# Last expert's second GEMM by seven products of halves, and S4 over 8 blocks of 256 samples

## The chip, the cores and the metric

The kernel runs on one core of one Trainium2 chip. The metric is the device time of one execution in microseconds. TensorE (PE) multiplies, VectorE (DVE) and ScalarE (ACT) do element-wise work, and GpSimd (POOL) and SyncE (SP) issue most DMAs. Each engine works through its own instructions in program order.

## The reference

The input x (2048 tokens by 512) is normalised to xn. The output is x plus a long convolution of xn (S4) plus a mixture of 8 experts on xn, in which all 8 experts are used for every token (top-8 of 8):

```python
def _A_ref(u, A_re, A_im, B_re, B_im, C_re, C_im, log_dt, Dskip):
    ...
    K = jnp.einsum("dn,dnl,dn->dl", Cc, P, dB).real      # 512 channels, 2048 samples, N = 128
    ...
    return y + u * Dskip                                  # y: causal convolution of u with K
def _B_ref(x, w_gate, w1, w2):
    ...
    for e in range(E):                                    # E = 8, D = 512, F = 1792
        h = _silu(xf @ w1[e]) @ w2[e]
        out = out + w * h                                 # w: softmax gate of the expert
x = A_u
xn = _layernorm(x, axis=-1)
return x + _A_ref(xn, ...) + _B_ref(xn, B_w_gate, B_w1, B_w2)
```

## The kernel before, in words

Each fp32 operand of a GEMM is split into a high and a low fp16 part, and each product is three fp16 matmuls (high·high, high·low, low·high). ACT makes the high part, and DVE the low part from it.

The work runs over experts e = 0..7, token blocks tb = 0..3 of 512 tokens, and four groups d of F (`DQS`: three groups of two pairs `pr`, one group of one pair; a pair is 256 of the 1792 columns). One (e, tb, d) is a call of `block`, which has four turns (`slot`, s = 0..3), so that a block of tokens has 16 turns.

- **First GEMM** (`product`, L1371, result `hb`): already seven products of halves per pair, 128x256 matmuls. Between them ACT copies one PSUM tile into another, which then accumulates on: `S.copy(B, A)` after turn 0 (L1605), `S.copy(C, B)` after turn 1 (L1615). Two of the four quarters of the result are finished by a copy to SBUF (`keep`, L1600) and an adding DMA on POOL's queue (`add`, L1571).
- **Activation** (`activate`): ACT takes the silu of a quarter (L1387) and makes the high part `ahl` (L1391); DVE makes the low part (L1400). Then the quarter stands in the list `units`.
- **Second GEMM** (`pop`, L1354 to L1356, result `y`): a unit is 2 x 3 matmuls of 128x512. `slot` takes `pops` units a turn from the list, behind the first GEMM's products of that turn. Four PSUM banks y0..y3 hold the four 128-token rows of a token block, and `evacuate` scales them by the gate and adds them to DRAM (`oacc`) by an adding DMA.
- **Weights** (`work_on`): list of steps that load, sum and split the next expert's w1 and w2, in the turns of the last token block of an expert and after it.
- **S4** runs beside all this. The 2048 samples of 16 channels (a chunk; 32 chunks) are 16 blocks of 128 samples. Per chunk: DVE builds tables (`s4_tables`, L769 to L775) from a basis made every second chunk (`s4_basis`), PE makes the kernel's samples (`s4_kernel`, L787), PE transforms kernel and input along the 128 samples (`s4_kf` L858, `s4_uf` L845), DVE multiplies and sums over the pairs of blocks (`s4_conv`, L884 to L898), PE transforms back (`s4_back`, L918), ACT reads it (`s4_out`, L925). DVE's share of it is issued by a budget: in each turn (`bg_run`) as many steps as 0.92 of the planned PE time leaves, less what DVE has otherwise. PE's share follows at fixed distances in turns (`until`, `hold`). What is not issued by the first turn of (7, 3), that is expert 7 and its last token block, is issued there in one go (`bg_until("s4")`), since its result is added from that block on (`s4_final`).
- **End**: after the last `block` the remaining units are popped, and `evacuate` combines the last four rows with what was loaded from `oacc` and sends them out by two queues.

The order of all instructions is written out by the program itself (a manual schedule): a turn, a list or a budget decides what is issued next, and the chip then runs each engine's instructions in that order.

Of the kernel before, what the change touches and what calls it, by code (L numbers as in the profile page):

```python
# [18 lines left out]
P = 128  # L19
# [14 lines left out]
def s4_moe_kernel(  # L34
# [205 lines left out]
    def x_sums(g, a):  # L240
# [90 lines left out]
    def x0_high(k):  # L331
        hi = xs_["hi"] = sb.tile([P, 4, TH], F16, tag="ta", name=f"x0h{k}", bufs=1)
# [51 lines left out]
    def gates_squares(row):  # L384
        gsq = sb.tile([P, KT * E], F32, tag="s4p1", bufs=1, name="gsq")
        S.activation(gsq, wgt.rearrange("p k e -> p (k e)"), AF.Square, accum_out=row)

    def gates_split():
# [3 lines left out]
        wgf = sb.tile([P, 6, E], F32, tag="s4p2", bufs=1, name="wgf")  # L392
# [142 lines left out]

    class Item:


        def __init__(self, load, steps, ready):
            self.load, self.steps, self.ready, self.raw, self.at = load, steps, ready, None, 0  # L540
            self.sums, self.n = len(steps) == 3, len(steps)
# [3 lines left out]
    live = {"n": 0, "tw": False}  # L545
# [4 lines left out]
    def piece_w1(e, pr, ready, raw=None):  # L550
# [6 lines left out]
        it.raw, it.made = raw, (e, "w1", pr)  # L557
        return it
# [6 lines left out]
    def piece_end(e, w, n, ready):  # L565
# [9 lines left out]
        def can_go():  # L575
            if "at" not in st:
                return ready()
            return now() > st["at"] + 1 and bank_free() and now() + 1 not in turns
# [18 lines left out]
    def can(it):  # L597
# [5 lines left out]
        if it.sums and len(it.steps) == it.n:  # L603
            return not live["tw"]
# [4 lines left out]
    def work_on(limit):  # L609
        while limit > 0:  # L610
# [15 lines left out]
            if it.sums and len(it.steps) == it.n:  # L626
                live["tw"], it.at = True, now()
# [6 lines left out]
            if low:  # L634
                lows.append((low, last, it.sums and last, it.made))
# [7 lines left out]
    def work_lows():  # L643

        while lows:
# [5 lines left out]
            if sums:  # L651
                live["tw"] = False
# [5 lines left out]
    ZSH = 18  # L658

    def s4_dft_load():  # L660
        s4["dft"] = sb.tile([P, 4, P], F32, tag="tb", name="dft", bufs=1)
        nc.sync.dma_start(s4["dft"], dft)

    def s4_dft():

        dftt = s4["dft"]
        times(dftt[:, 2:4, :], dftt[:, 2:4, :], DSH)
        V.tensor_copy(dfth[:, 0], dftt)
        V.tensor_tensor(dfth[:, 1], dftt, dfth[:, 0], op=ALU.subtract)

    def s4_dt():
        xx = [sb.tile([P, D], F32, tag=t, name=f"dtx{n}", bufs=1) for n, t in enumerate(("k4", "ta", "tt"))]
# [3 lines left out]
    upad = cp.tile([P, 2, DC, NI + 1], F32, name="upad")  # L676
# [4 lines left out]
    def s4_raw(g):  # L681
        raw = sb.tile([P, 6, GD], F32, tag="s4raw", name=f"s4raw{g}", bufs=2)
# [3 lines left out]
    def s4_basis(g):  # L686
# [3 lines left out]
        wv = sb.tile([P, 2, GD], F32, tag="s4w", name=f"s4w{g}", bufs=2)  # L690
        db = sb.tile([P, 2, GD], F32, tag="s4db", name=f"s4db{g}", bufs=1)
        p1 = sb.tile([P, 2, GD], F32, tag="s4p1", name=f"s4p1{g}", bufs=1)
        p2 = sb.tile([P, 2, GD], F32, tag="s4p2", name=f"s4p2{g}", bufs=1)
        at = sb.tile([P, 2, GD], F32, tag="s4at", name=f"s4at{g}", bufs=1)
# [12 lines left out]
        n4 = [P, 2, NK, DC]  # L707
# [6 lines left out]
        f = sb.tile(n4, F32, tag="b0", name=f"bf{g}", bufs=1)  # L714
        r = sb.tile(n4, F32, tag="b1", name=f"br{g}", bufs=1)
        x = sb.tile(n4, F32, tag="b2", name=f"bx{g}", bufs=1)
        zr = sb.tile(n4, F32, tag="zr", name=f"zr{g}", bufs=1)
        zi = sb.tile([P, 2] + n4[1:], F32, tag="zi", name=f"zi{g}", bufs=1)
# [23 lines left out]
        s4["basis", g] = (wv, zr, zi)  # L742
        yield 2 * tt_(352) + 0.3

    def s4_tables(c):
        g, h = c // 2, c % 2
        wv, zr, zi = s4["basis", g]
        tb = sb.tile([P, 2, 3, DC, 32], F32, tag="tb", name=f"tb{c}", bufs=1)
# [3 lines left out]
        for st in range(6):  # L752
# [9 lines left out]
            n4 = [P, 2, nn, L]  # L762
            zrv = zr[:, h, k0:k0 + ns, :].rearrange("p k d -> p (k d)").unsqueeze(1).unsqueeze(3).to_broadcast(n4)
            ziv = zi[:, :, h, k0:k0 + ns, :].rearrange("p c k d -> p c (k d)").unsqueeze(3).to_broadcast(n4)
            ta = sb.tile([P, 1024], F32, tag="ta", name=f"ta{c}_{st}", bufs=1)[:, :2 * nn * L]
            ta = ta.rearrange("p (c n l) -> p c n l", c=2, n=nn)
            tt = sb.tile([P, 1024], F32, tag="tt", name=f"tt{c}_{st}", bufs=1)[:, :2 * nn * L]
            tt = tt.rearrange("p (c n l) -> p c n l", c=2, n=nn)
            V.tensor_tensor(ta, tin, zrv, op=ALU.mult)  # L769
            if st > 2:  # L770
                yield tt_(2 * nn * L)
            V.tensor_tensor(tt, tin[:, ::-1], ziv, op=ALU.mult)
            if st > 2:
                yield tt_(2 * nn * L)
            V.tensor_tensor(tout, ta, tt, op=ALU.add)  # L775
            yield (1 if st > 2 else 3) * tt_(2 * nn * L) + 0.5 * (st == 0)
# [15 lines left out]
    def s4_kernel_out(c):  # L792
        ksb = sb.tile([P, 4, 4, NI], F32, tag="ksb", name=f"ksb{c}", bufs=1)
# [5 lines left out]
        kt = sb.tile([P, DC, NI], F32, tag="kt", name=f"kt{c}", bufs=1)  # L799
# [7 lines left out]
    def s4_kscale(c):  # L807


        ks = s4["ks", c] = sb.tile([P, 2], F32, tag="ksc", name=f"ksc{c}", bufs=4)  # L810
        pow2_scale(ks[:, 0:1], s4["kst", c], f"k{c}")
        pow2_inverse(ks[:, 1:2], ks[:, 0:1], ZSH - DSH)

    def s4_khigh(c):
        kh = s4["kh", c] = sb.tile([P, 2, DC * NI], F16, tag="kh", name=f"kh{c}", bufs=1)
# [8 lines left out]
    def s4_uload(c):  # L824

        uc = sb.tile([P, NI, DC], F32, tag="uc", name=f"uc{c}", bufs=1)
        nc.sync.dma_start(uc, xnd[:, :, c * DC:(c + 1) * DC])
        s4["uc", c] = uc.rearrange("p i d -> p d i")

    def s4_uhigh(c):  # L830
        uh = s4["uh", c] = sb.tile([P, 2, DC, NI], F16, tag="uh", name=f"uh{c}", bufs=1)
# [6 lines left out]

    def s4_uf(c):
        uh = s4["uh", c]  # L840
        take_bank()
        uf = ps_s.tile([P, 2, DC, NI], F32, tag="s4", name=f"uf{c}")
        for a in range(2):
            for n, (x, y) in enumerate(((0, 0), (1, 0), (0, 1))):
                T.matmul(uf[:, a].rearrange("p d i -> p (d i)"), dfth[:, x, a, :], uh[:, y].rearrange("p d i -> p (d i)"),  # L845
                         start=(n == 0), stop=(n == 2))
        clock["pe"] += 0.66
# [4 lines left out]
    def s4_kf(c):  # L852
        take_bank()
        kf = ps_s.tile([P, 2, DC, NI], F32, tag="s4", name=f"kf{c}")
        kh = s4["kh", c]
        for a in range(2):
            for n, (x, y) in enumerate(((0, 0), (1, 0), (0, 1))):
                T.matmul(kf[:, a].rearrange("p d i -> p (d i)"), dfth[:, x, 1 - a, :], kh[:, y], start=(n == 0), stop=(n == 2))  # L858
        clock["pe"] += 0.66
        k4 = sb.tile([P, 4, DC, NI], F32, tag="k4", name=f"k4{c}", bufs=1)  # L860
        S.copy(k4[:, 0:2].rearrange("p a d i -> p (a d i)"), kf.rearrange("p a d i -> p (a d i)"))
        bank["at"] = now()
        s4["k4", c] = k4

    def s4_conv(c):

        up, k4 = upad, s4["k4", c]
        v3 = sb.tile([P, 3, DC, NI], F32, tag="v3", name=f"v3{c}", bufs=1)
        V.scalar_tensor_tensor(v3[:, 2], up[:, 1, :, 0:NI], sgnt[:, 1:2], up[:, 0, :, 1:], op0=ALU.mult, op1=ALU.add)
# [905 lines left out]
```

## Time and profile before

| | |
|---|---|
| median of 3 runs | 2326.76 us (2326.36 to 2327.77) |
| profiled execution | 2325.2 us from the first to the last instruction |
| PE busy | 2312.5 us, 99% |
| DVE busy | 1961.5 us, 84% |
| ACT busy | 1464.8 us, 63% |
| POOL busy | 341.3 us, 15% |
| HBM | 202.14 MB read, 66.06 MB written |
| mean granted TensorE clock | 0.999 |

The profiled execution's own time and the median of the runs are 1.6 us apart. PE's busy time counts every matmul until its result has landed, so that neighbouring matmuls overlap: a 128x256 matmul has a duration of 273 ns, but the next one starts sooner. What a matmul costs in a row of them is read from starts.

The part of the span at the end: the first GEMM's last matmuls start at 2303.05 us, the second GEMM's remaining units follow from 2304.36 us on, its last matmul starts at 2320.98 us, and the span ends at 2325.2 us.

### The profile page before, as it was taken

What the parts mean: (1) busy time and instruction counts of PE and PEld (TensorE: products, weight loads), DVE (VectorE), ACT (ScalarE), POOL (GpSimd) and SP (SyncE); (2) the same over time, 40 slices, a digit from 0 to 9 for tenths busy, and PEclk for the clock granted to TensorE, in tenths of its full rate; (3) what the DMA queues carried; (4) which work ended last, traced back from release to release, by engine and by line L of the source; (5) the groups of instructions that cost most, each with busy time, mean ns of one, the idle gap of its engine ahead of it and who ended that gap; (6) DMA issues with size and microseconds to landing.
All of it is one profiled execution on the core that took longest, in us unless ns stands there. A gap on an engine that the chain in (4) does not pass through costs nothing.

```text
span 2325.2 us, 45209 instructions
## 1 busy us (share of the span) xinstructions
PE 2312.5 (99%) x17701; PEld 1539.0 (66%) x17701; DVE 1961.5 (84%) x3810; ACT 1464.8 (63%) x2584; POOL 341.3 (15%) x395
## 2 busy tenths in 40 slices
PE   8999999999999999999999999999999999999999
PEld 4666666666666666666666666666666666666665
DVE  8854877989998999999899979999889997998611
ACT  7676665657666576665766657666576665764443
POOL 0000101121111111111111111111111110111112
PEclk9999999999999999999999999999999999999999
DMA  7696456575566655645556546564565654543447
GB/s 281 191 269 186 121 138 147 130 157 129 128 155 153 144 134 127 153 106 112 146 113 147 117 110 150 124 140 105 117 155 112 145 128 93 150 95 61 83 88 177
DMA packets 327686, 320.72 MB, mean 138 GB/s; under 512 B 183664, under 2 KB 220016, under 8 KB 327024
## 3 DMA queue, kind: packets, MB, share of 16 engines
q1 hardware_dynamic: 271024, 223.70, 31.7%
q0 software_dynamic: 55872, 93.61, 25.6%
q8 instruction: 138, 2.26, 0.4%
q14 instruction: 76, 0.62, 0.1%
q10 hardware_dynamic: 576, 0.52, 0.1%
HBM read 202.14 MB, written 66.06 MB: 115 GB/s over the span
## 4 chain that ended last, share of the span: by engine, by line
PE 98%; DMA 1%; DVE 0%; ACT 0%; SPq 0%; issue 0%; DVEq 0%; ACTq 0%
PE hb L1371 43%; PE y L1355 17%; PE y L1356 17%; PE y L1354 17%; PE kgen L787 1%; PE kf L858 1%; PE yp L918 1%; PE uf L845 1%; PE hb L1662 1%; PE tp L288 0%; DMA ut<-in_u_dram 0%; DMA w2s<-in_w_dram 0%; DMA xnd<-xn 0%; DMA f<-in_w_dram 0%; DMA ut0b<-in_u_dram 0%; DMA raw<-in_w_dram 0%
## 5 line engine op out<-in xcount | busy, mean ns | idle before, releaser
L1371 PE MATMUL hb<-xop,w1s 128*128 128x256 f16 x9114 | 1072.8, 273 | 0.0
L1371 PEld LDWEIGHTS <-w1s 128*128 128x128 f16 x9114 | 885.4, 98 | 173.3 <-issue 0.8
L1355 PE MATMUL y<-w2s,ahl 128*128 128x512 f16 x1792 | 679.2, 379 | 0.6 <-DVE w2s L509 0.6
L1356 PE MATMUL y<-w2s,ahl 128*128 128x512 f16 x1792 | 679.2, 379 | 0.0
L1354 PE MATMUL y<-w2s,ahl 128*128 128x512 f16 x1792 | 679.2, 379 | 0.0
L1356 PEld LDWEIGHTS <-ahl 128*128 128x128 f16 x1792 | 175.3, 98 | 212.2 <-issue 0.9
L1571 POOL DMA_DIRECT2D scC<-sE x124 | 118.2, 953 | 1266.2 <-ACT sE L1600 1082.6
L890 DVE TENSOR_TENSOR s<-s,tm 128x720 f32<-128x720 f32 (+14 forms) x480 | 268.9, 560 | 16.6
L1354 PEld LDWEIGHTS <-ahl 128*128 128x128 f16 x1792 | 175.3, 98 | 161.5
L1355 PEld LDWEIGHTS <-ahl 128*128 128x128 f16 x1792 | 175.3, 98 | 161.3
L1387 ACT ACTIVATE fa<-hb,sc 128x512 f32<-128x512 f32 (+1 forms) x252 | 160.4, 637 | 189.2 <-PE hb L1371 188.7
L889 DVE TENSOR_TENSOR tm<-v,k 128x720 f32<-128x720 f32 (+14 forms) x480 | 267.5, 557 | 10.7
L1400 DVE SCALAR_TENSOR_TENSOR ahl<-fa,sc,ahl 128x512 f16<-128x512 f32 (+1 forms) x262 | 178.7, 682 | 63.4 <-ACT ahl L1391 63.1
L1615 ACT COPY hb<-hb 128x512 f32<-128x512 f32 x124 | 64.1, 517 | 229.7 <-PE hb L1371 229.4
L1391 ACT ACTIVATE ahl<-fa,sc 128x512 f16<-128x512 f32 (+1 forms) x262 | 175.8, 671 | 9.8 <-DMA xnd<-xn 0.9
L1571 POOL DMA_DIRECT2D scB<-sE x124 | 107.1, 864 | 437.9 <-ACT scB L1600 324.0
L1605 ACT COPY hb<-hb 128x512 f32<-128x512 f32 x124 | 64.3, 519 | 168.3 <-PE hb L1371 167.7
L1400 DVE SCALAR_TENSOR_TENSOR ahl<-scB,sc,ahl 128x512 f16<-128x512 f32 x124 | 84.4, 680 | 77.4 <-ACT ahl L1391 76.0
L1400 DVE SCALAR_TENSOR_TENSOR ahl<-scC,sc,ahl 128x512 f16<-128x512 f32 x124 | 84.2, 679 | 67.6 <-ACT ahl L1391 64.0
L775 DVE TENSOR_TENSOR tb<-ta,tt 128x64 f32<-128x64 f32 (+2 forms) x192 | 131.9, 687 | 5.5
L769 DVE TENSOR_TENSOR ta<-tb,zr 128x64 f32<-128x64 f32 (+2 forms) x192 | 131.6, 686 | 5.4
L1332 POOL DMA_DIRECT2D oacc<-ye x108 | 95.9, 1334 | 244.7 <-ACT ye L1328 243.1
(252 smaller groups left out, 2447.2 us busy)
## 6 DMA issues: line engine op xcount, KB each, us to landing
xop<-xd SPq DMA_DIRECT2D x210, 256.0 KB, 3.8
pp<-in_w_dram SPq DMA_DIRECT2D x98, 512.0 KB, 4.4
raw<-in_w_dram SPq DMA_DIRECT2D x56, 512.0 KB, 4.8
oacc<-ye POOLq DMA_DIRECT2D x108, 256.0 KB, 6.2
scC<-sE POOLq DMA_DIRECT2D x93, 256.0 KB, 4.2
scB<-sE POOLq DMA_DIRECT2D x93, 256.0 KB, 4.2
raw<-in_w_dram SPq DMA_DIRECT2D x52, 256.0 KB, 4.2
raw<-in_w_dram SPq DMA_DIRECT2D x104, 128.0 KB, 4.1
```

Source lines behind the costliest of these rows:

```text
L769: V.tensor_tensor(ta, tin, zrv, op=ALU.mult)
L775: V.tensor_tensor(tout, ta, tt, op=ALU.add)
L889: V.tensor_tensor(tm, v3f[:, :, 0:n], kb, op=ALU.mult)
L890: V.tensor_tensor(s3[:, :, m:], s3[:, :, m:], tm, op=ALU.add)
L1354: T.matmul(y, lhs[0], w2s[pr][:, 0, fh, :], start=(c == 0), stop=False)
L1355: T.matmul(y, lhs[0], w2s[pr][:, 1, fh, :], start=False, stop=False)
L1356: T.matmul(y, lhs[1], w2s[pr][:, 0, fh, :], start=False, stop=(c == NF - 1))
L1371: T.matmul(dst[:, q, :], w1s[pr][:, a, wo, k * P:(k + 1) * P], xop[:, xo, b, k, :], start=(first_mm and q == 0 and n == 0), stop=(n == 5), ...
L1387: S.activation(fa, src[:, :n], AF.Silu, scale=w1_unscale(e, d if whole else prs[0]))
L1391: S.activation(ahl[:, 0, :n], fa, AF.Copy, scale=scales[e][:, 3:4])
L1400: V.scalar_tensor_tensor(ahl[:, 1, :n], fa, sc[:, 3:4], ahl[:, 0, :n], op0=ALU.mult, op1=ALU.subtract)
L1571: nc.gpsimd.dma_start(dst, src, accum_op=ALU.add)
```

## The change: what it does

- **Second GEMM of expert 7 by seven products of halves.** For 256 tokens (th) and a pair, the two halves of the tokens, of F and of D make quarters; seven products with sums of quarters take the place of eight. A product is three 128x256 matmuls; one `pop2` is 21 of them. The sums and splits of the activations (`prep_sums`, `prep_high`, `prep_low`) come in three stages of an item (e, tb, th, d), one stage a turn, the first stage of the next item in the same turn as the last of the one before. Items of a token block run th = 1 first, then th = 0. A half token block uses all four banks y0..y3; `read` (or `read_last`) combines the banks.
- **The weights w2 of expert 7** are summed and split as well (`piece_w2x`, `w2_load`, `w2_sums`), into a tile `w2x` beside `w2s`.
- **S4 over 8 blocks of 256 samples.** The transform has a radix-2 step: four groups of three 128x128 matmuls in place of two groups of three 128x256 ones, with `butterfly` additions on DVE around a sum over 8 blocks on twice as many rows.
- **S4's buffers in a pool `sp` that closes ahead of the last token block of expert 6** (`second_open` at (6, 3)), where `bg_until("s4")` now stands; a pool `p2` for the last expert opens in its place. Tables, chunks and bases run as three streams beside each other (`s4_tabs`, `chunks`, `bases`), and `s4_pe` issues whichever of its four kinds of steps is due. The tables' steps are smaller (512 elements).
- S4's results of tokens 1024 to 2047 are added at (7, 2), the others at (7, 3). Input and output of a chunk go by four DMAs each in place of one.

The core of the diff (moves of tiles from `sb` or `cp` to `sp` are left out):

```diff
+    def prep_sums(k):
+        ...
+        V.tensor_tensor(sums[:, 0, :n], a21, a22, op=ALU.add)
+        V.tensor_tensor(sums[:, 1, :n], sums[:, 0, :n], a11, op=ALU.subtract)
+        V.tensor_tensor(sums[:, 2, :n], a11, a21, op=ALU.subtract)
+        V.tensor_tensor(sums[:, 3, :n], a12, sums[:, 1, :n], op=ALU.subtract)
+    def prep_parts(k, n, q0, q1, sums):
+        pl, st = open_[k]
+        return ((pl[:, :, :n, 0, :], q0[:, :n, :P]),
+                (pl[:, :, :n, 1:3, :].rearrange("p a q s t -> p a q (s t)"), q1[:, :n]),
+                (st[:, :, :, :n], sums[:, :, :n]))
+    def prep_high(x):
+        ...
+        for dst, src in prep_parts(*x):
+            S.activation(dst[:, 0], src, AF.Copy, scale=scales[x[0][0]][:, 3:4])
+    def prep_low(x):
+        ...
+        for dst, src in prep_parts(*x):
+            V.scalar_tensor_tensor(dst[:, 1], src, scales[e][:, 3:4], dst[:, 0], op0=ALU.mult, op1=ALU.subtract)
+        for q, pr in enumerate(DQS[d]):
+            units2.append((k, q, pr, now()))
+    def prep():
+        if pipe["at"]:
+            step, x = pipe["at"]
+            if step:
+                prep_low(x)
+                pipe["at"] = None
+            else:
+                prep_high(x)
+                pipe["at"] = (1, x)
+        if pipe["at"] is None and order and len(open_) < ring(order[0][:2]):
+            k = order[0]
+            if all((*k, f) in quarters and quarters[(*k, f)][1] < now() for f in range(2)):
+                order.pop(0)
+                pipe["at"] = (0, prep_sums(k))
+    def pops2(n):
+        pipe["owed"] = min(pipe["owed"] + n, 2)
+        while pipe["owed"] > 0 and units2 and units2[0][3] < now() and not units:
+            ...
+            pop2()
+            pipe["owed"] -= 1
+    def pop2():
+        ...
+        for b, h, fa, ia, fb, ib in SEQ:
+            for n, (x, y) in enumerate(((0, 0), (0, 1), (1, 0))):
+                lhs = st[:, x, ia, q, :] if fa else pl[:, x, q, ia, :]
+                T.matmul(ys[key][b][:, h], lhs, (wx, ws)[fb][:, y, ib, :], ...)
+    def read_sums(y, w, u):
+        S.copy(w[:, 0], y[0][:, 0])
+        V.tensor_tensor(u[:, 0], y[0][:, 1], w[:, 0], op=ALU.add)
+        V.tensor_tensor(u[:, 1], y[3][:, 0], u[:, 0], op=ALU.add)
+        V.tensor_tensor(w[:, 1], y[2][:, 1], u[:, 0], op=ALU.add)
+    def read(e, tb, th, y):
+        ...
+        read_sums(y, w, u)
+        V.tensor_tensor(o, y[2], u[:, 1:2, :].to_broadcast([P, 2, TH]), op=ALU.add)
+        V.tensor_tensor(w, y[1], w, op=ALU.add)
+        ...
+    def read_last(e, tb, th, y):
+        ...
+        read_sums(y, w, u)
+        V.scalar_tensor_tensor(o[1], u[:, 1:2, :].to_broadcast([P, 2, TH]), g[1], o[1], ...)
+        V.scalar_tensor_tensor(o[0], w, g[0], o[0], op0=ALU.mult, op1=ALU.add)
+        for j in (1, 0):
+            for h, q in ((0, nc.sync), (1, nc.scalar)):
+                V.scalar_tensor_tensor(o[j][:, h], y[1 + j][:, h], g[j], o[j][:, h], ...)
+                q.dma_start(out[...], o[j][:, h])
     def slot(e, tb, d, s, pops):
...
-        pop(pops)
+        if e >= E2:
+            if units:
+                pop(min(3, len(units)))
+            pops2(pops)
+        else:
+            pop(pops)
         flush()
+        if e >= E2:
+            prep()
...
+        if e >= E2:
+            reads()
         clock["slot"] += 1
     def block(e, tb, d):
...
+        if d == 0 and e >= E2:
+            order.extend((e, tb, th, g) for th in (1, 0) for g in range(len(DQS)))
+        elif e >= E2:
+            pops = (1, 0, 1, 0) if last else (1, 1, 1, 1)
...
-            if e == E - 1 and tb == NB - 1:
+            if (e, tb) == (E2 - 1, NB - 1):
                 bg_until("s4")
+                second_open()
...
-    units.sort(key=lambda x: x[6])
-    n1 = sum(x[6] for x in units)
-    pop(len(units) - n1)
-    ...
+    while units2 or order or pipe["at"]:
+        pops2(1)
+        prep()
+        reads()
+        clock["slot"] += 1
+    reads()
+    def transform(dst, src, row):
+        for a in range(2):
+            for o in range(2):
+                for n, (x, y) in enumerate(((0, 0), (1, 0), (0, 1))):
+                    T.matmul(dst[:, a, o], dfth[:, x, 4 * o + row(a), :], src[:, y, o], ...)
+    def butterfly(dst, src):
+        V.tensor_tensor(dst[:, :, 0:DC], src[:, :, 0:DC], src[:, :, DC:], op=ALU.add)
+        V.tensor_tensor(dst[:, :, DC:], src[:, :, 0:DC], src[:, :, DC:], op=ALU.subtract)
     def s4_conv(c):
...
-        for m in range(NI):
-            n = NI - m
+        for m in range(NB2):
+            n = NB2 - m
...
+        yield from together([chunks(), s4_tabs(), bases()])
```

More of the change, by code (lines that the diff above doesn't have):

```diff
@@ L634, in work_on @@
             if low:
-                lows.append((low, last, it.sums and last, it.made))
+                lows.append((low, last, it.lane if it.sums and last else None, it.made))
             elif last and it.load is not None:
@@ L837, in s4_ulow @@
         V.tensor_tensor(uh[:, 1], s4["uc", c], uh[:, 0], op=ALU.subtract)
+    def transform(dst, src, row):
+        dst = dst.rearrange("p a (o d) i -> p a o d i", o=2)
+        for a in range(2):
+            for o in range(2):
+                for n, (x, y) in enumerate(((0, 0), (1, 0), (0, 1))):
+                    T.matmul(dst[:, a, o], dfth[:, x, 4 * o + row(a), :], src[:, y, o], start=(n == 0), stop=(n == 2))
+        clock["pe"] += 0.68
     def s4_uf(c):
@@ L841, in s4_uf @@
         take_bank()
[L842 to L847, printed above, removed]
+        uf = ps_s.tile([P, 2, 2 * DC, NB2], F32, tag="s4", name=f"uf{c}")
+        transform(uf, uh, lambda a: a)
         S.activation(upad[:, :, :, 1:].rearrange("p a d i -> p (a d) i"), uf.rearrange("p a d i -> p (a d) i"),
@@ L853, in s4_kf @@
         take_bank()
[L854 to L861, printed above, removed]
+        kf = ps_s.tile([P, 2, 2 * DC, NB2], F32, tag="s4", name=f"kf{c}")
@@ L1020, in s4_pe, with act_free @@
+        while any(cs for _, cs, _ in left):
+            it = next((x for x in left if x[1] and x[2](x[1][0])), None)
+            if it is None or not bank_free():
+                yield None
+                continue
+            c = it[1].pop(0)
+            it[0](c)
+            yield None
+            if it[0] is kernel:
+                yield from bank_wait()
+                yield from until(("ke", c))
         yield from bank_wait()
         done.add("s4")
+    def act_free():
+        while clock["actleft"] + clock["act0"] - clock["act"] - clock["conv"] < 0.0:
+            yield None
@@ L1073, in s4_dve, with s4_tabs @@
             polled.append(s4_zsplit(c))
+    def s4_tabs():
+        for c in range(NCH):
+            if c:
+                yield from until(("kn", c - 1), more=0)
+            yield from until(("basis at", c // 2), more=-1)
+            yield from s4_tables(c)
+            s4["tab", c] = now()
     def s4_x(c):
@@ L1411, in s4_moe_kernel, with reads @@
+    def reads():
+        if "send" in pipe and pipe["send"][0] < now():
+            pipe.pop("send")[1]()
+        while pipe["out"]:
+            pipe["out"].pop(0)()
     older = []
```

476 lines of the change are left out of this document (300 added, 176 removed).

## The prediction

> **What bounds the kernel now.** I read the granted clock, the page's busy times, who waits for whom on PE, the chain that ended last, and then the timeline of the last 30 us.
>
> ```profile
> core 0: 2325.2 us, clock 0.999
> PE 2312.5 (99%) x17701; PEld 1539.0 (66%) x17701; DVE 1961.5 (84%) x3810; ACT 1464.8 (63%) x2584; POOL 341.3 (15%) x395
> PE tot_a L178 <- DVE row L1178: 6.9, 1, 6.9
> PE hb L1164 <- POOL ident masks.py:199: 1.4, 1, 1.4
> PE y L1355 <- DVE w2s L509: 0.6, 1, 0.6
> PE 98%; DMA 1%; DVE 0%; ACT 0%; SPq 0%; issue 0%; DVEq 0%; ACTq 0%
> PE hb L1371 43%; PE y L1355 17%; PE y L1356 17%; PE y L1354 17%; PE kgen L787 1%; PE kf L858 1%; PE yp L918 1%; PE uf L845 1%; PE hb L1662 1%; PE tp L288 0%; DMA ut<-in_u_dram 0%; DMA w2s<-in_w_dram 0%; DMA xnd<-xn 0%; DMA f<-in_w_dram 0%; DMA ut0b<-in_u_dram 0%; DMA raw<-in_w_dram 0%
> ```
>
> The three waits are all that PE has in the whole run, and the last of them lies at 39 us. From there to 2321 us PE runs without a gap, at full clock. So matmul columns taken away count in full, less DVE work counts for nothing, and every new wait of PE counts in full too. That last point decides here.
>
> ```profile
> 2290.84 2.62 PE hb L1371 x24
> 2304.36 0.38 PE L1354 MATMUL y<-w2s,ahl 128*128 128x512 f16 x1
> ...
> 2320.98 0.38 PE L1356 MATMUL y<-w2s,ahl 128*128 128x512 f16 x1
> 2321.40 0.88 DVE L1338 SCALAR_TENSOR_TENSOR fin<-y,gse,fin 128x256 f32<-128x256 f32 x2 [1.07 <-PE y L1356]
> ```
>
> A 128x256 matmul in a row of them takes 2.62/24 = 0.1092 us. From the first to the last of these starts are 77 steps (13 units of 6 matmuls): 16.62/77 = 0.2158 us for 128x512. G = 2304.36 is the end of the first GEMM. Behind it come 16.8 us of PE work and, from PE's end at 2321.2 to 2325.2, 4.0 us of read and store.
>
> **Term 1, the second GEMM of expert 7: -16.6 us.** Before: 56 pairs of (th, pr) with 12 matmuls, 672 x 0.2158 = 145.0. After: 56 `pop2` of 21 x 0.1092 = 2.29 us, 128.4. No bound apart: the first GEMM runs the same form 9114 times.
>
> **Term 2, S4's transforms: +1.4 us.** Twelve 128-column matmuls in place of six of 256, three times a chunk, 96 times in all. Nearest row: transposes, 128 columns, each with its own weight load.
>
> ```profile
> 172.51 0.61 PE L288 MATMUL tp<-ident,xl 128*128 128x128 f16 x8
> 172.96 0.38 PE L1354 MATMUL y<-w2s,ahl 128*128 128x512 f16 x1
> L288 PEld LDWEIGHTS <-xl x84: 97/98/98, 60.1 to 178.4; 128*128 128x128 f16 x84
> ```
>
> Eight take 0.45 us, 0.056 each, though a load is shown with 98 ns: loads overlap each other. So 12 x 0.056 - 6 x 0.1092 = 0.017, or 1.6 at most over 96; I take 1.4. Upper end: if each waited for its own 98 ns load, 12 x 0.098 - 0.655 = 0.52, times 96 is +50. The Trainium skill, "TensorE: Matmul & The Clock Gate", section "Back-to-back issue gap", gives about 81 ns for N = 128 in a stream of load and matmul pairs; by it the term would be an estimated +30 us. The trace's 56 ns disagrees, and the same section's 131 ns for N = 512 disagrees with 215.8 here.
>
> **Term 3, new waits of PE inside expert 7: +17 us.** `prep` handles an item in three turns and starts the next with the third: one item per two turns. An item gives two `pop2` (one for d = 3), and `pops2` needs its stamp to be older than the turn. By the turns in the diff: the first item of (7, 0) is summed in turn 5, split in 6 and 7, popped in 8; th = 1 items can start only in turns 5, 9, 13, 17, th = 0 items then in 19, 21, 23, 25, and the next token block's follow without a break. So two pops stand in every second (even) turn, and mostly none in the odd ones. What they covered:
>
> ```profile
> 2297.84 1.47 PE L1371 MATMUL hb<-xop,w1s 128*128 128x256 f16 x12
> 2299.15 0.38 PE L1354 MATMUL y<-w2s,ahl 128*128 128x512 f16 x1
> 2299.35 0.36 ACT L1615 COPY hb<-hb 128x256 f32<-128x256 f32 x1 [0.80 <-PE hb L1371]
> L1615 ACT COPY hb<-hb 128x512 f32<-128x512 f32 x93 | 53.0, 570 | 207.1 <-PE hb L1371 206.9
> L871 DVE TENSOR_TENSOR v<-v 128x256 f32<-128x256 f32 x32 | 13.6, 425 | 1.1
> L769 DVE TENSOR_TENSOR ta<-tb,zr 128x512 f32<-128x512 f32 x32 | 22.1, 690 | 1.0
> L1400 DVE SCALAR_TENSOR_TENSOR ahl<-fa,sc,ahl 128x256 f16<-128x256 f32 x62 | 29.7, 478 | 5.1 <-ACT ahl L1391 5.1
> L1400 DVE SCALAR_TENSOR_TENSOR ahl<-scB,sc,ahl 128x512 f16<-128x512 f32 x93 | 69.5, 747 | 60.6 <-ACT ahl L1391 59.2 <-ACT st_k L173 1.2
> L509 DVE SCALAR_TENSOR_TENSOR w1s<-tw,sc,w1s 128x1024 f16<-128x1024 f32 x54 | 69.1, 1279 | 12.6 <-ACT w1s L506 12.6
> ```
>
> The copy of turn 1 starts 0.20 us after PE's next matmul could, and takes 0.57 (0.36 for d = 3). Turn 2 begins with a product that adds onto the copied tile. In the old order y matmuls lay between; with no pop in turn 1, PE waits some 0.83 us (0.62). In (7, 0): turns 4 and 5 (no item ready), 9 and 13: 3.1 us. In each of the other blocks two or three such turns: 2.5, 1.7, 1.7.
>
> At the change of banks from th = 0 to the next block's th = 1 there is more: `read` stands on DVE ahead of the next item's low parts. Pop's end, 0.20, copy 0.36, three sums of 0.425, two of 0.690, then low parts of 256, 512, 1024: 0.478 + 0.747 + 1.279 = 2.50. Together 5.7 us, against 2.6 us of d = 3 products in turns 29 and 30. The first matmuls of the pop need no last part, so about 2.7 us of wait, three times: 8.1. Sum 3.1 + 5.9 + 8.1 = 17. At the change inside a block (turn 20 to 22) 5.2 us of products cover it. Bounds: 0 if every wait finds a pop in front; 25 if (7, 0) is held up longer by w2's extra sums and splits.
>
> **Term 4, the end: +16 us.** The same rate leaves items (1,1) done and (1,2), (1,3), (0,0) to (0,3) undone at G: 12 pops, 27.5 us of PE work (10.7 more than before, which the first GEMM's end gains: no loss). But it lies bare.
>
> ```profile
> 2305.47 0.86 POOL L1571 DMA_DIRECT2D scB<-sE  x1 [1.76 <-ACT scB L1600]
> 2308.31 0.49 ACT L1387 ACTIVATE scB<-scB,sc 128x256 f32<-128x256 f32 x1
> L1391 ACT ACTIVATE ahl<-fa,sc 128x256 f16<-128x256 f32 x62 | 31.5, 508 | 2.0
> L1391 ACT ACTIVATE ahl<-fa,sc 128x512 f16<-128x512 f32 x200 | 144.3, 722 | 7.8 <-DMA xnd<-xn 0.9 <-ACT fa L1387 0.4
> L506 ACT ACTIVATE w1s<-tw,sc 128x1024 f16<-128x1024 f32 x54 | 61.7, 1143 | 0.4 <-DVE tw L519 0.4
> L372 PE MATMUL tp<-ident,xhl x32: 219/314/314, 11.7 to 15.1; 128*128 128x128 f16 x32
>   ACT xhl L358: 7.1, 1
> ```
>
> (a) ACT's high parts of (1,2) stand behind the last two silus, which wait for the adding DMA: done at G + 4.0 to 4.4. High 0.51 + 0.72 + 1.14, last low 1.28: (1,2) is ready at about G + 7.8; PE has only (1,1), 4.6 us. Wait 3.2. (b) At the change to th = 0 `read_last` stands ahead of the low parts of (0,0): 0.20 + 0.36 + 3 x 0.425 + 2 x 0.747 + 4 x 0.478 + 2.50 = 7.7, wait 7.3. (c) After such an idle time PE is slow: after 7.1 us of waiting at the start 128-column matmuls took 314 ns in place of 219, from 11.7 to 15 us, 32 in 3.3 us, half the pace. 3.3 us at half pace lose 1.7. The Trainium skill, same page, section "Part 1: The HAM clock gate", states that a window of about 3.4 us idle halves the clock; these rows agree. (d) After PE's last matmul `read_last` again, 5.2 us in place of two 0.48 steps: +4.1. Between items DVE needs 4 x 0.425 + 1.14 + 1.28 = 4.3 us with the hand-overs, PE 4.6: no wait. Sum 16.3. Bounds 9 (without a and half of b) and 22.
>
> **Work that costs nothing, and its cover.**
>
> ```profile
> 2237.30:2304.36 67.06, 67.06 (x457) 44.61 (x456) 10.11 (x15) 31.17 (x54) 24.06 (x28) 1.00 0.80 170
> 170.00:2237.30 2067.30, 1813.69 (x3473) 1.00 0.56 129
> L889 DVE TENSOR_TENSOR tm<-v,k 128x720 f32<-128x720 f32 (+14 forms) x480 | 267.5, 557 | 10.7
> L890 DVE TENSOR_TENSOR s<-s,tm 128x720 f32<-128x720 f32 (+14 forms) x480 | 268.9, 560 | 16.6
> L889 DVE TENSOR_TENSOR tm<-v,k 128x672 f32<-128x672 f32 x32 | 27.3, 854 | 0.5
> ...
> L889 DVE TENSOR_TENSOR tm<-v,k 128x96 f32<-128x96 f32 x32 | 8.2, 258 | 1.1
> L769 DVE TENSOR_TENSOR ta<-tb,zr 128x1024 f32<-128x1024 f32 x64 | 78.2, 1222 | 1.6
> L898 DVE TENSOR_TENSOR z<-s x32: 415/418/421, 399.4 to 2195.5; 128x256 f32<-128x256 f32 x32
> L926 SPq DMA_DIRECT2D ys<-ysb x32: 525/566/1572, 432.5 to 2230.6; - x32
> ```
>
> The first row is the stretch of (7, 3): DVE 10.1, ACT 31.2 of 67.1 us. The items add per block some 26 us to DVE and 7 to ACT: neither is full. The extra w2 sums and splits (7 x 3.8 us of DVE) fall where S4 is over.
>
> S4 has to be done at (6, 3) now. Per chunk: sums fall from 30 instructions to 14 (seven sizes from 672 to 96, 7.8 us in place of 536.4/32 = 16.8, by the page's groups L889 and L890), six butterflies add 2.6, twelve 512-element steps for six of 1024 add 0.9: -5.5, and 32 x 5.5 = 176. An expert without S4 is 4 x 67.06 = 268 us of PE and 76 of DVE (4 x 10.1, and 7 pairs' weights at 5.1), so DVE has 1814 - 176 - 76 = 1562 us of work in 2067 - 268 = 1799: 87%, against 88% before, when the last sum came 42 us ahead of its place. So it fits about as before, without much to spare: 0. The lighter DVE gives nothing, since PE never waits for it. SP issues six more DMAs a chunk, 0.57 each: 109 us spread over 1800; POOL's eight adds of S4 that move to (7, 2) go past no add that PE needs within 4 us.
>
> **Sum.** 2325.2 - 16.6 + 1.4 + 17 + 16.3 = 2343.3. The median of the runs is 1.6 above the profiled execution: 2345.
>
> **The rivals.**
> 1. *The preparation runs an item ahead.* If (say, through late weights in (7, 0)) a finished item stands in the list at each turn, pops come one a turn, the waits of turn 1 and of the bank changes lie under pops, and (a) goes: -16.6 + 1.4 + 3 + 11 = -1.2, 2325.6; if the low parts of (0,0) also stand ahead of the read, 2.5 less of (b), and with its idle time short the slow clock goes: 2321. It decides from one spare item on. For it: the old order kept PE without a wait by a list always filled. Against: production and use have the same rate, and nothing builds a stock but the two turns of d = 3 without a pop. This is the side of faster or same, 2316 to 2330.
> 2. *S4 misses its place.* Three streams with fixed distances in turns have to get through a chunk in 1799/32 = 56 us; if 5% of the turns find none due, some 50 us of DVE work is issued in one go at (6, 3) with PE waiting: 2360 to 2390. For it: 87% against a budget of 92%. Against: the streams no longer wait for each other.
> 3. *The 128-column matmuls are bound by their loads.* +30 to +50: 2375 to 2395. Against: the transposes.
>
> **How the numbers follow.** Forecast as summed 0.55 (own range 2335 to 2355); rival 1 0.30 (faster 0.18, within 0.2% 0.12); rival 2 0.11; rival 3 0.04. 0.2% is 4.7 us, about what a measurement of this kernel can tell. From the forecast's low bounds (0 of term 3 and 9 of term 4) 0.02 each go to faster and same. Faster 0.20, same 0.14, slower 0.66. The range 2319 to 2366 leaves out the lower part of rival 1 and the upper of 2 and 3.
>
> **What would show it.** Term 1: z matmuls, 1176, 0.109 apart. Term 2: kf, uf and yp starts 0.056 apart. Term 3: PE waits for ACT's copy L1615 in expert 7, and for DVE's low parts at the bank changes. Term 4: some 48 us from the last hb to the end with one gap of 7 us and a granted clock under 1 behind it. S4: its last yp ahead of about 1970 us. Wrong if PE shows no waits after 1970 us.

## The result, and the profile after

The kernel after takes 2352.66 us (median of 4 runs, 2351.68 to 2354.85), the kernel before 2327.26 us beside it (4 runs, 2326.36 to 2327.77). The ratio is 1.0111, 95% interval 1.0097 to 1.0125: 25.4 us slower, where 2345 was predicted. The profiled execution has 2350.6 us.

The clock row, two lines of the page (busy time, and the chain that ended last), and who waits for whom on PE:

```profile
core 0: 2350.6 us, clock 0.997
```
```profile
PE 2309.1 (98%) x18781; PEld 1598.6 (68%) x18781; DVE 1877.6 (80%) x3914; ACT 1500.4 (64%) x2631; POOL 342.2 (15%) x395
...
PE 96%; DVE 1%; ACT 1%; DMA 1%; issue 0%; SPq 0%; DVEq 0%; ACTq 0%
```
```profile
PE hb L1466 <- ACT hb L1894: 9.0, 14, 0.7
PE z L1613 <- DVE st L1569: 7.4, 7, 1.4
...
PE z L1613 <- DVE pl L1569: 5.3, 5, 3.2
...
PE z L1613 <- ACT pl L1563: 1.2, 1, 1.2
PE z L1613 <- DVE w2s L518: 1.2, 1, 1.2
PE uf L906 <- ACT ysb L1000: 1.0, 1, 1.0
PE hb L1466 <- ACT hb L1884: 1.0, 1, 1.0
```

PE is less busy by 3 us, DVE by 84, and the run is longer. Before, three rows held all waits of PE, and the last was over at 39 us; the two of the start are as they were and left out here. New are waits for ACT's copy (L1894, turn 1; one of the 14 lies in expert 6's time), for DVE's low parts `pl` and `st` (L1569) and for ACT's high parts (L1563). `z` is the second GEMM's result in the kernel after. These rows count from the end that the profile models for a matmul. What a wait costs is read from starts: the distance to the next start, less the usual 0.1092 us. By that measure the copy wait of a full group costs 0.88 us and not 0.71.

The timeline of PE and of what it waits for, at five places: a pop that needs new weights, a turn 1, a change of banks between two token blocks, the first wait behind the first GEMM, and the change to th = 0 at the end.

```profile
2114.75 1.28 DVE L518 SCALAR_TENSOR_TENSOR w2s<-tx,sc,w2s 128x1024 f16<-128x1024 f32 x1
...
2116.08 1.03 PE L1613 MATMUL z<-w2s,st 128*128 128x256 f16 x8 [1.19 <-DVE w2s L518]
...
2140.02 0.57 ACT L1894 COPY hb<-hb 128x512 f32<-128x512 f32 x1 [3.95 <-PE hb L1466]
...
2140.64 1.58 PE L1466 MATMUL hb<-xop,w1s 128*128 128x256 f16 x13 [0.71 <-ACT hb L1894]
...
2156.50 0.68 DVE L1641 TENSOR_TENSOR o<-z,o 128x512 f32<-128x512 f32 x1
...
2157.10 0.48 DVE L1569 SCALAR_TENSOR_TENSOR pl<-q,sc,pl 128x256 f16<-128x256 f32 x1
...
2157.64 0.28 PE L1613 MATMUL z<-w2x,pl 128*128 128x256 f16 x1 [0.56 <-DVE pl L1569]
...
2159.49 0.72 PE L1613 MATMUL z<-w2s,st 128*128 128x256 f16 x5 [1.36 <-DVE st L1569]
...
2309.24 0.51 ACT L1527 ACTIVATE scB<-scB,sc 128x256 f32<-128x256 f32 x1 [3.12 <-DMA scB<-sE]
...
2310.20 0.80 PE L1613 MATMUL z<-w2x,pl 128*128 128x256 f16 x3 [1.21 <-ACT pl L1563]
...
2319.74 0.37 ACT L1626 COPY wu<-z 128x256 f32<-128x256 f32 x1 [1.26 <-PE z L1613]
...
2322.67 1.65 DVE L1665 SCALAR_TENSOR_TENSOR fin<-z,gse,fin 128x256 f32<-128x256 f32 x4
...
2324.77 0.40 PE L1613 MATMUL z<-w2x,pl 128*128 128x256 f16 x1 [3.21 <-DVE pl L1569]
```

In each the releaser stands in brackets, and the row above it shows what stood in its way: at 2114 the low part of expert 7's own weights, at 2157 `read` (L1641 is its last step) ahead of the low part, at 2309 a silu that waits for the adding DMA, at 2322 `read_last`.

The granted clock in five stretches of PE's work, each right behind such waits, three behind changes of banks and two at the end. A row has the stretch and its length, then busy time and number of instructions of PE, PEld, DVE, ACT and POOL, then the granted clock (third number from the end), the DMA share and GB/s:

```profile
2159.49:2163.00 3.51, 3.51 (x22) 2.67 (x22) 3.32 (x7) 1.67 (x2) 0.85 (x1) 0.65 0.99 133
2230.02:2234.00 3.98, 3.98 (x37) 3.58 (x38) 3.79 (x7) 1.67 (x2) 1.16 (x2) 1.00 1.09 283
2298.88:2302.00 3.12, 3.12 (x29) 2.80 (x30) 2.93 (x7) 1.67 (x2) 0.83 (x1) 1.00 1.00 165
...
2313.17:2318.00 4.83, 4.83 (x29) 3.63 (x30) 3.89 (x11) 2.40 (x4) 0.00 (x0) 0.65 0.22 66
2326.63:2330.87 4.24, 4.24 (x20) 3.02 (x21) 4.01 (x8) 2.16 (x3) 0.00 (x0) 0.50 0.00 0
```

Three of the five are slow: behind the first change of banks and twice at the end. In them matmuls start 0.213 us apart in place of 0.109, some 55 in all.

### The profile page after: what moved, and what is told of

Its sections match the earlier page's. It is cut to its first block, busy times and chain, and to the rows that moved or that the text cites. A ratio compares the mean times of both kernels' runs of the same rounds, so it can differ in the third digit from the quotient of the medians.

```text
span 2350.6 us, 47857 instructions
## 1 busy us (share of the span) xinstructions
PE 2309.1 (98%) x18781; PEld 1598.6 (68%) x18781; DVE 1877.6 (80%) x3914; ACT 1500.4 (64%) x2631; POOL 342.2 (15%) x395
## 3 DMA queue, kind: packets, MB, share of 16 engines
q0 software_dynamic: 55872, 93.61, 25.4%
## 4 chain that ended last, share of the span: by engine, by line
PE 96%; DVE 1%; ACT 1%; DMA 1%; issue 0%; SPq 0%; DVEq 0%; ACTq 0%
PE hb L1466 42%; PE y L1450 14%; PE y L1451 14%; PE y L1449 14%; PE z L1613 5%; PE hb L1942 2%; PE kgen L845 1%; PE uf L906 1%; PE kf L906 1%; PE yp L992 1%; DMA scB<-sE 0%; DVE st L1569 0%; PE tp L297 0%; ACT hb L1894 0%; ACT st L1563 0%
## 5 line engine op out<-in xcount | busy, mean ns | idle before, releaser
L1451 PE MATMUL y<-w2s,ahl 128*128 128x512 f16 x1568 | 594.3, 379 | 0.0
L1450 PE MATMUL y<-w2s,ahl 128*128 128x512 f16 x1568 | 594.3, 379 | 0.0
L1449 PE MATMUL y<-w2s,ahl 128*128 128x512 f16 x1568 | 594.3, 379 | 0.0
L1451 PEld LDWEIGHTS <-ahl 128*128 128x128 f16 x1568 | 153.4, 98 | 185.0 <-issue 0.2
L1450 PEld LDWEIGHTS <-ahl 128*128 128x128 f16 x1568 | 153.4, 98 | 140.8
L1449 PEld LDWEIGHTS <-ahl 128*128 128x128 f16 x1568 | 153.4, 98 | 140.7
L1482 ACT ACTIVATE fa<-hb,sc 128x512 f32<-128x512 f32 (+1 forms) x220 | 140.2, 637 | 135.7 <-PE hb L1466 135.2
L1894 ACT COPY hb<-hb 128x512 f32<-128x512 f32 x124 | 64.3, 518 | 227.1 <-PE hb L1466 226.8
L1495 DVE SCALAR_TENSOR_TENSOR ahl<-fa,sc,ahl 128x512 f16<-128x512 f32 (+1 forms) x230 | 157.1, 683 | 49.0 <-ACT ahl L1486 48.4
L1486 ACT ACTIVATE ahl<-fa,sc 128x512 f16<-128x512 f32 (+1 forms) x230 | 154.4, 672 | 8.1 <-ACT fa L1482 0.4
L833 DVE TENSOR_TENSOR tb<-tb,pt 128x512 f32<-128x512 f32 (+3 forms) x256 | 141.6, 553 | 5.4
L829 DVE TENSOR_TENSOR pt<-tb,zi 128x512 f32<-128x512 f32 (+3 forms) x256 | 141.3, 552 | 5.5
L830 DVE TENSOR_TENSOR tb<-tb,zr 128x512 f32<-128x512 f32 (+3 forms) x256 | 140.4, 548 | 0.0
L961 DVE TENSOR_TENSOR s<-s,tm 128x672 f32<-128x672 f32 (+6 forms) x224 | 127.8, 570 | 7.7
L960 DVE TENSOR_TENSOR tm<-v,k 128x672 f32<-128x672 f32 (+6 forms) x224 | 126.3, 564 | 2.5
```

The lines of the kernel that those rows point to most:

```text
L829: V.tensor_tensor(pt, tin[:, ::-1, r], ziv, op=ALU.mult)
L830: V.tensor_tensor(tout[:, :, r], tin[:, :, r], zrv, op=ALU.mult)
L833: V.tensor_tensor(tout[:, :, r], tout[:, :, r], pt, op=ALU.add)
L961: V.tensor_tensor(s3[:, :, m:], s3[:, :, m:], tm, op=ALU.add)
L1449: T.matmul(y, lhs[0], w2s[pr][:, 0, fh, :], start=(c == 0), stop=False)
L1450: T.matmul(y, lhs[0], w2s[pr][:, 1, fh, :], start=False, stop=False)
```

## The experiments

The theory: what the change costs beyond its own arithmetic is waits of PE, and these come from the order in which the engines' work is issued, not from a lack of DVE or ACT time. The rivals stand with each run. Gains below are against the 2352.66 us of the kernel after; the kernel before had a median of 2327.05 us beside the first four and 2327.2 to 2327.3 beside the others.

**The old second GEMM with the new S4.**

```diff
-    E2 = E - 1
+    E2 = E
-            if (e, tb) == (E2 - 1, NB - 1):
+            if (e, tb) == (E - 2, NB - 1):      # S4's pool still closes at (6, 3)
     ...                                         # end and s4_final as before
```

> Expert 7's second GEMM, its weights and the end of the kernel are those of before; S4 stays as changed (8 blocks of 256 samples, done ahead of (6, 3)). Theory (the loss lies in expert 7's turns and the end; S4 costs only its 128-column matmuls, 1.6 us, and two single waits of PE that the changed kernel's trace shows, 1.2 and 0.8 us): 2329 to 2332 us. Rival (squeezing S4 into one expert less makes DVE or ACT late, and costs part of the 25 us): 2336 us or more, with waits of PE on DVE's low parts before (6, 3).

Measured: 2329.61 us, ratio 1.0011 (1.0002 to 1.0020), span 2328.8. Beside the start-up waits of before, PE has two waits:

```profile
PE uf L906 <- ACT ysb L1000: 1.3, 1, 1.3
PE hb L1466 <- ACT hb L1895: 0.6, 1, 0.6
```

So S4's 8 blocks cost about 2.5 us (0.5 to 4.7 by the interval; 3.6 between the profiled spans): two waits in 1800 us, and some 1.6 for the transforms. S4 neither misses its place nor runs into its weight loads, and the other 23 us belong to the second GEMM of expert 7, with its weights and the end.

**One pop a turn.**

```diff
-        pipe["owed"] = min(pipe["owed"] + n, 2)
+        pipe["owed"] = min(pipe["owed"] + n, 1)
```

> At most one pop2 a turn (the owed pops are capped at 1, not 2). Theory (PE waits for ACT's copy of turn 1 because the two pops stand in the even turns): the pops of an item fall on both turns, 7 of the 14 waits of 0.88 us go (those of turns 9, 17, 25, 37, 41, 53 and 57 of expert 7), -6 us, 2346 to 2348. Rival (ACT is too busy in expert 7 and the copy is late whatever lies between): the waits stay, 2351 to 2354.

Measured: 2343.34 us, 9.3 less, ratio 1.0068 (1.0055 to 1.0080).

```profile
PE hb L1466 <- ACT hb L1894: 4.0, 7, 0.7
```

The copy waits fell from 14 to 7, as expected. The extra 3 us were not. Part of the wait at the change to th = 0 went as well (from 3.38 + 1.35 to 1.68 + 0.41 by starts), since the pop that ends th = 1 comes later when the pops are spread, and the low parts of item (0,0), from 2309.97 to 2312.6, now stand ahead of the read, from 2313.46 on. In the first block a wait of 1.35 for weights went and one of 1.15 for the copy of turn 0 came.

**PE kept busy in the two waits of the end.** 36 and 44 matmuls into a bank that nobody reads are added ahead of the first pops of (1,2) and (0,0).

```diff
+        if (e, tb, q) == (E - 1, NB - 1, 0) and (th, d) in ((1, 2), (0, 0)):
+            keep_busy(36 if th else 44, xop[:, 0, 0, 0, :])
```

> 36 and 44 matmuls of 128x256 whose result is not used are put ahead of the first pop of item (1,2) and of item (0,0) of the last token block, where PE waits anyway; 3.9 and 4.8 us of work in waits of 4.4 and 5.2. Theory (behind these waits the granted clock is down to half and a matmul takes 0.21 us in place of 0.109, which costs 5.8 us at the end): the clock stays at 1, -5 us, 2347 to 2349. Rival (the slow matmuls come from DVE and ACT reading PSUM or SBUF at the same time): the pace stays at 0.21 us, 2352 to 2355.

Measured: 2349.45 us, ratio 1.0091 (1.0077 to 1.0105): 3.2 less, though PE has 80 matmuls more. The clock of the end, and of a change of banks ahead of it that the edit doesn't touch:

```profile
2313.00:2318.00 5.00, 4.21 (x39) 3.72 (x39) 4.73 (x12) 1.92 (x4) 0.00 (x0) 1.00 0.18 56
...
2324.00:2330.00 6.00, 5.77 (x53) 4.94 (x52) 5.76 (x10) 3.28 (x5) 0.00 (x0) 1.00 0.16 55
...
2297.86:2301.06 3.20, 3.20 (x17) 2.27 (x15) 3.01 (x6) 1.15 (x1) 0.00 (x0) 0.50 1.07 204
```

At the end the clock stays at 1.00, so the slow clock there follows from the waiting. It is worth more than the 3.2 us: the added matmuls take 8.7 us and waits of 1.35 are left, where the kernel after waits 8.5, and by starts its slow clock at the end costs 4.1. The last row shows the slow clock at a change of banks, where the kernel after had 1.00 (its row for 2298.88 above): which of the changes is hit differs from one execution to the next (the last section shows by what).

**Low parts ahead of the read at a change of banks.**

```diff
+    def lows_first():
+        if pipe["out"] and pipe["at"] and pipe["at"][0]:
+            n = len(units2)
+            prep_low(pipe["at"][1])
+            units2[n:] = [(*x[:3], x[3] + 1) for x in units2[n:]]
+            pipe["at"] = None
     ...
+            lows_first()       # ahead of reads(), in slot and in the loop at the end
             reads()
```

> At a change of banks the next item's low parts are issued on DVE ahead of the read of the banks, not behind it. Theory (the low parts stand behind the read on DVE, and PE waits for them): 2.25 us at each of three changes between token blocks falls to about 1, 1.35 at the change inside (7, 0) to about 0, and the 4.7 us at the last change to about 2: -6 to -8 us, 2344 to 2347. Rival (the read only takes the low parts' place as what PE waits for): 2351 to 2354.

Measured: 2340.80 us, ratio 1.0058 (1.0045 to 1.0070): 11.9 less.

```profile
PE z L1613 <- DVE st L1569: 2.4, 4, 1.1
...
PE z L1613 <- DVE pl L1569: 0.4, 1, 0.4
```

The waits for low parts drop from 12.7 us to 2.8. By starts, the three changes of banks lose all of their 2.25 us each, the change to th = 0 goes from 4.7 to 1.9, and with the waiting goes 3.3 us of slow clock, which the expectation had left out and which puts the time below its 2344. The wait of 1.35 us in (7, 0) stayed, against the expectation: it is for weights.

**The last silus behind the split.**

```diff
+    pops2(1)
+    prep()
+    reads()
+    clock["slot"] += 1
     while later:
         later.pop(0)()
```

> Behind the last block's first GEMM one round of pop, split and read is issued before the last two silus, so ACT splits item (1,2) without standing behind the silus that wait for the adding DMA. Theory (term 4a: that order costs the wait for (1,2), 3.8 us, and these short waits bring on the slow clock of 2313 to 2318 us, 35% of 4.8 us = 1.7): the waits of 1.37, 1.02 and 1.09 us at 2309 to 2312 shrink below 1 in sum, the clock there stays near 1, total 4 to 5.5 less, 2347 to 2349. Rival (the DMA is what holds the end: item (1,3) needs the same silus one item later): the wait moves to (1,3), 2351 to 2353.

Measured: 2347.19 us, ratio 1.0085 (1.0072 to 1.0099): 5.5 less. Nothing is left of the waits at 2309 to 2313, and (1,3) does not inherit them. The stretch up to the change to th = 0 has the full clock; the one behind the change is slow as before:

```profile
2306.00:2317.00 11.00, 11.00 (x103) 9.87 (x101) 7.17 (x17) 7.25 (x13) 1.73 (x2) 1.00 0.74 192
...
2323.00:2327.00 4.00, 4.00 (x25) 2.98 (x23) 3.77 (x8) 2.16 (x3) 0.00 (x0) 0.60 0.00 0
```

**Expert 6's rest spread over the turns.**

```diff
-                pop(min(3, len(units)))
+                pop(min(1, len(units)))
```

> In expert 7 the rest of expert 6's y work is given out one unit a turn where it was three. Theory (the waits of 1.15, 0.88 and 0.88 us in the first block's turns 3 to 9 lie bare only because that rest is used up in the first turns): these three waits go, 2.9 us, 2349 to 2350.5; the waits of the other blocks and of the end stay. Rival (these waits come from the first items being late, so that the same time lies bare a few turns on): 2352 to 2353.

Measured: 2346.23 us (2341.93 to 2350.48), ratio 1.0079 (1.0067 to 1.0092): 6.4 less, about twice what was expected.

```profile
PE hb L1466 <- ACT hb L1894: 6.9, 11, 0.7
...
PE z L1613 <- ACT ye L1423: 1.6, 1, 1.6
```

The three waits went. A new one came, for the banks of expert 6 (`ye` is its evacuation, later now); of five waits in (7, 0) for items and weights one is left, and a copy wait of the second block fell away. In the first two blocks the waits go from 10.7 to 6.5 us by starts. The wait for item (1,2) at the end grew by 1.3. The profiled execution also has no slow stretch in the blocks and no wait of `uf`, which the edit doesn't touch; how much of the 6.4 us is such luck, this run can't tell.

**All four together.**

> All four reorderings together: one pop a turn, the low parts ahead of the read at a change of banks, the last silus behind the split, expert 6's rest spread. Theory (all that the change lost is waits whose cover was taken away by the order, and the order can give it back: -16.6 for the second GEMM, +1.6 transforms, +1.9 S4's two waits, then some 4 of waits left in the first block, 2 at its in-block change, 2 to 6 at the end): 2322 to 2330, the turn-1 waits for the copy gone but for one or two in the first block. Rival (the waits were slack of ACT and DVE that lack rate for one item per two turns: without them PE waits for the items instead): 2334 or more, with PE waiting for DVE's low parts in each block.

Measured: 2331.48 us (11 runs), ratio 1.0019 (1.0010 to 1.0028): 21.2 less, and 1.5 above the range expected. The waits for DVE's low parts that the rival needs are absent. The copy waits of the d = 3 turns stayed, 0.66 in each block, against the expectation. PE's waits, and the timeline of a new one:

```profile
PE hb L1466 <- ACT hb L1902: 7.3, 8, 2.0
PE z L1613 <- DVE fin L1665: 1.8, 1, 1.8
PE z L1613 <- ACT ye L1423: 1.6, 1, 1.6
...
PE z L1613 <- DVE wu L1627: 1.2, 1, 1.2
```
```profile
2152.24 1.80 POOL L1649 DMA_DIRECT2D oacc<-o  x2 [8.47 <-ACT o L1647]
2153.72 1.21 POOL L1850 DMA_DIRECT2D scC<-sE  x1
...
2162.02 0.51 ACT L1527 ACTIVATE scC<-scC,sc 128x256 f32<-128x256 f32 x1 [5.33 <-DMA scC<-sE]
...
2164.49 0.57 ACT L1902 COPY hb<-hb 128x512 f32<-128x512 f32 x1
...
2165.11 2.78 PE L1466 MATMUL hb<-xop,w1s 128*128 128x256 f16 x24 [1.93 <-ACT hb L1902]
```

The two adds of a read (L1649) come onto POOL's queue just ahead of the add to `scC`, in the short turns of d = 3. The silu behind that add waits 5.3 us on ACT, and PE's copy stands behind the silu. This cost 2.10 and 2.18 us at two changes of blocks, and the end still had 1.41 and 1.99 us at the change of banks, with a slow clock behind them.

**And the waits that were left.** In addition a read's rows are sent three turns later; the last half block uses three banks of the first GEMM, free by then; and of `read_last` for th = 1 only the steps that free bank y0 stand ahead of the next item.

```diff
-        if "send" in pipe and pipe["send"][0] < now():
+        if "send" in pipe and pipe["send"][0] < now() - 3:
     ...
+            if (e, tb, th) == (E - 1, NB - 1, 0):
+                ys[key][1:] = hb
     ...
+        if th:
+            pipe["rest"] = rest       # issued behind the last prep_low
+        else:
+            rest()
```

> The four reorderings together, and three more at the waits that they left: the scaled rows of a read are sent three turns later, behind the adds that the next block's first silu needs (PE waited 2.10 and 2.18 us for ACT's copy, which stood behind that silu); the last half block (th = 0 of the last token block) takes three of the first GEMM's banks, free by then, and only the first two steps of the read before it stand ahead of the next item's sums, the rest behind the last split (1.41 and 1.99 us, and the slow clock behind them from 2307 to 2311). Theory (the order alone is what the change lost): -4.3, -3.4 and about -2, so 2320 to 2324, ratio 0.997 to 0.999, granted clock 1.00 to the end, waits of expert 7 below 6 us in sum. Rival (the rate of DVE and ACT at the end is the limit): the waits come back between the last items, 2328 or more.

Measured: 2321.15 us (10 runs, 2320.59 to 2323.46) against 2327.30: ratio 0.9975, 0.9966 to 0.9985. This is faster than both kernels. PE's waits, without one of 1.4 us at the start that all kernels here have:

```profile
PE tot_a L187 <- DVE row L1273: 7.3, 1, 7.3
PE hb L1466 <- ACT hb L1913: 3.3, 6, 0.7
PE z L1615 <- ACT ye L1423: 1.6, 1, 1.6
```
```profile
2282.75:2300.00 17.25, 17.25 (x160) 15.46 (x158) 15.87 (x31) 12.43 (x22) 3.52 (x4) 1.00 0.76 167
2300.00:2312.50 12.50, 12.50 (x117) 11.15 (x114) 10.25 (x24) 2.94 (x5) 0.00 (x0) 1.00 0.13 42
2312.50:2319.20 6.70, 0.22 (x3) 0.00 (x0) 3.65 (x8) 0.00 (x0) 0.00 (x0) 0.70 0.23 80
```

PE works through the whole end at full clock (the last row lies behind its last matmul), and the items keep up with it: DVE and ACT had the time, though DVE is busy for 15.9 of the 17.25 us in the first row. Of the 31.5 us against the kernel after, 21.2 are by order alone; what the three banks and the two other steps are worth apart was not measured. Against before, the span is 6.0 us shorter (2319.2): -16.6 for the matmuls, +1.6 for the transforms, +6.0 for the waits that are left (0.8 in S4's time, 1.7 for `ye`, 3.5 for copies), and +2.7 behind PE's last matmul make -6.3.

## Why the prediction was right, point by point

It said slower by 18 us; it is 25, inside its own range of 2335 to 2355 and near the upper end. The direction and the place were right, and two terms were too small (term 3, and S4's place). The working below is by starts of the profiled execution.

**Term 1, -16.6: held.** The four forms of `z` matmuls, 504 + 336 + 168 + 168, are 1176, and they lie 0.109 apart in undisturbed stretches (three of them in 0.33 us from 2319.21 on).

**Term 2, +1.4: held, at 1.4 to 1.6.** Twelve of S4's 128-column matmuls take from 1966.47 to 1967.14, 0.056 each:

```profile
1966.47 0.83 PE L992 MATMUL yp<-zh,dfth 128*128 128x128 f16 x12
1967.14 1.47 PE L1466 MATMUL hb<-xop,w1s 128*128 128x256 f16 x12
...
1972.34 0.93 PE L1466 MATMUL hb<-xop,w1s 128*128 128x256 f16 x7
```

Rival 3 is out. The Trainium skill's 81 ns (the section that the prediction named) again disagrees with the trace, here for S4's own matmuls.

**S4's place: 0 in the prediction, 1.9 measured.** The last `yp` comes 5 us ahead of (6, 3)'s first product at 1972.34, so rival 2 is out. DVE has 1546 us of work in the 1802 us from 170 to 1972 (86%; 87% was forecast) and PE waits for none of it. The two short waits, 1.2 us at 798 and 0.8 us at 1815, are both for ACT, which the step did not look at: at 798 ACT's read of `yp` stands behind a silu that waits 2.1 us for an adding DMA, and at 1815 the copy of turn 1 stands behind S4's steps on ACT, the last of them 0.63 us at 1814.32.

**Term 3, +17: 23.9 measured. This is the step that was mis-sized.**
- Turns of (7, 0) without an item: 3.6 in place of 3.1 (1.15, 0.88, 0.88, and 0.66 for d = 3).
- Pops of (7, 0) held up: 3.8, in five waits. Four of them are for w2's splits or for an item behind these on ACT and DVE, the longest 1.35 (2116.08 above) and 1.30 (an item's `st`); the fifth, 0.39 at 2087.62, has no split of w2 in its way. The prediction had this in its upper bound and left it out of the sum.
- Copy waits of the other blocks: 8.1 in place of 5.9 (seven of 0.88, three of 0.66): a turn more than counted in each.
- Changes of banks between blocks: 3 x 2.25 in place of 3 x 2.7. The wait comes in two parts (0.72 for `pl`, 1.52 for `st`), because a pop starts with its `pl` products.
- The change of banks inside a block: no wait, "covered" as forecast. (What an expectation above calls a wait at the in-block change is the one at 2116.08; its releaser shows that it is for the weights.)
- A slow clock behind the first change of banks: 1.7, not in the term at all.

**Term 4, +16.3: 14.8 measured**, with errors of up to 2.6 us that cancel: that the sum comes so close is luck.
- (a) 3.8 in place of 3.2, as told.
- (b) 4.7 in place of 7.3. `read_last` began at 2319.74, 1.6 us ahead of the end of the pop's last matmul, since bank y0 is complete early. From there to the end of the three low parts it took 6.8 us in place of 7.5, and PE did five matmuls of the new pop ahead of the third low part: it goes on at 2324.77 with the first low part and waits 1.35 us more for the third, until 2326.63.
- (c) 4.1 in place of 1.7: the clock fell twice at the end, and first behind a row of waits of which the longest was 1.4 us. The prediction expected it behind the long wait alone.
- (d) 2.2 in place of 4.1: the last read starts early for the same reason as in (b).

Sum: -16.6 + 1.6 + 1.9 + 23.9 + 14.8 = 25.6, against 25.4 between the two profiled spans.

**Rival 1** (the preparation runs an item ahead) did not come by itself, but its mechanism is what the experiments used: in the last run, with one pop in each turn and the low parts ahead of the read, PE waits for no item any more. That the waits are a matter of order was argued in the prediction from DVE's 10.1 us of 67 in (7, 3); the last two runs show it, the last of them with other banks for one half block.

## What to carry to other kernels

Where PE has no gaps, fewer matmuls pay only if the new work keeps covering PE's other waits: ask of each matmul that goes, or that moves to another turn, which copy or split it had hidden. A total of free time on DVE and ACT does not answer that; the order at each hand-over does (here 16.6 us of matmuls were gained, some 36 us of waiting and slow clock came in, and 31.5 us were won back without touching the arithmetic). When reads free the banks that PE wants next, put the next item's last split ahead of the read, or give PE other banks. Short waits close together cost twice: a step of 3.413 us with 2.04 us of waiting in it brought 1.7 us of slow clock (next section).

## What the runs showed of the hardware that was not expected

The clock falls behind short waits that add up, and not each time. A change of banks has waits of 0.72 and 1.52 us in 3.6 us of time. Five profiled executions have three such changes each with the same waits (the kernel after, and the runs with one pop a turn, added matmuls, later silus and spread units), and half pace followed 1, 2, 1, 1 and 0 times: in the clock rows, 0.65 and then twice 1.00 for the kernel after, 0.50 with the added matmuls.

The traces' records of the granted clock show what decides. In each execution the clock falls only at times on a grid of 3.413 us. In the kernel after it falls at 2160.53, 2314.13 and 2324.37 us, 45 and 3 steps of 3.413 us apart; with one pop a turn at 2154.33, 2290.87 and 2304.52 us, 40 and 4 steps apart. Here are PE's waits of expert 7, by starts, summed in each step of this grid ahead of the one in which PE ends, over the seven executions with the new second GEMM in which the clock falls before PE has ended (all but the last run's):

| step of the grid at full clock | how many | clock in the next step |
|---|---|---|
| 2.04 to 3.08 us of waiting | 13 | half, each time |
| 2.02 us of waiting or less | all others | full, each time |

So the waits of a change of banks count when they fall nearly whole into one step (2.04 us at the first change of the kernel after) and not when a step's end divides them (1.55 and 1.22 us at the second, with the copy wait ahead of it). Where the grid lies is luck of the execution. This is worked out from the traces; no run moved the waits against the grid on purpose.

A step at half pace is 15 or 16 matmuls of 0.213 us and costs 1.7 us, 12 to 14 matmuls where a wait reaches into it. A second one followed three times, each with another 1.0 to 1.7 us of waiting in the first; together they are 21 to 24 matmuls.

The Trainium skill ("TensorE: Matmul & The Clock Gate", section "Part 1: The HAM clock gate") states a free-running window of about 3.4 us. The grid and the length of the stretches agree. Its condition of an idle window would not lead one to expect a slow clock from 2.2 us of waiting; the traces decide here, and say that it happens.
